# Sliding-window attention and channel mix on one core: q and k turned by VectorE in 32x32 blocks, scores on 32-row groups, outputs of batches 2 to 7 turned by the crossbar

## The chip, the cores and the metric

The kernel runs on one core of a Trainium2 chip. The metric is the device time of one execution in microseconds (us). Three runs of the kernel before gave 235.13, 235.77 and 236.39 us; the median is 235.77.

The engines that matter here are TensorE (matmuls; PE in the profile, its weight loads PEld), VectorE (DVE), ScalarE (ACT), GpSimd (POOL, which here mostly issues loads that cast from float32 to bfloat16) and SyncE (SP, which issues stores and crossbar transposes). Each engine works through its own queue in order.

## What is computed

```python
# q, k, v: (8 batches, 8 heads, 576, 64) float32
scores = matmul(q, k.T) / sqrt(64)
rel    = pos[:, None] - pos[None, :]
bias   = 2.0 ** -(head + 1) * -abs(rel)
scores = where((rel >= 0) & (rel < 128), scores + bias, -1e9)
attn   = softmax(scores)
x      = matmul(attn, v)            # heads laid side by side: (8, 576, 512)
xp     = x moved down by one position, zero first
xk     = mu_k * x + (1 - mu_k) * xp
xr     = mu_r * x + (1 - mu_r) * xp
out    = sigmoid(xr @ w_r) * (relu(xk @ w_k) ** 2 @ w_v)    # 512 -> 1024 -> 512
```

## The kernel before, in words

All matmuls take bfloat16. The work has two halves that are interleaved: attention per batch b and head pair g (8 x 4), and the channel mix, which takes two batches P = b // 2 at a time (1,152 rows in chunks of 512, 384 and 256).

**Attention of one head pair.** A matmul contracts over partitions, so q and k are needed with the 64 head values on partitions, and they come from memory with positions on partitions. How they are turned depends on the batch:
- Batches 1 and 2: wide loads into `cb` (L463), 32 transposes of 64x64 blocks by TensorE per head pair into two PSUM banks (`qk_quad`, L1053), and two copies from PSUM to `qk` (L663, on ScalarE or VectorE).
- Batches 3 to 5: eight loads of one 128-position block each per batch, four for q and four for k (L498), transposes for two head pairs at a time (`qk_some` through `halves`, L804), and four copies on ScalarE.
- Batches 6 and 7: the same loads, then crossbar transposes issued by SyncE into `qx` (`flip`, L502).
- Positions 512 to 575 (the tails) are loaded apart into `ts` (L488) and turned by TensorE for batches 1 to 3 (L879, then a copy on VectorE) and by the crossbar from batch 4 on (`tail_flip`, L595).

Then `scores` (L693) computes, for the two heads of the pair, the scores of each key block against the queries that can see it. Each head lies on 64 partitions, so the two heads run on the two 64-row halves of the array. A pair gives two PSUM tiles `duo` of two banks (both that there are). ScalarE takes the exponential (L707), VectorE multiplies by a stored mask that holds bias and window (L720). `attend` (L749) multiplies by v, with a column of ones that gives the sums; VectorE takes the reciprocal (L755) and scales (L760) into `xu`, of which there are three.

**Turning the output.** The mix needs channels on partitions. For batches 0 to 5 TensorE transposes `xu` (`out_t`, L787) and ScalarE copies to `xt` (L663). For batches 6 and 7 SyncE issues a crossbar transpose from `xu` to `xt` (`out_flip`, L869). `shift` then forms on VectorE the difference of neighbours `dl` (L847) and the two mixes `xk` and `xr` (L854).

**Channel mix** (`channel_mix`): xk times w_k (L958), relu on ScalarE (L965), square (L931 on VectorE; for the first three chunks L929 on ScalarE is allowed too), xr times w_r (L976), tanh on ScalarE for the sigmoid (L983), the squares times w_v (L992), the product on VectorE (L997), and a store by SyncE (L1022).

**What sets the order.** The kernel's Python code holds a planner (class `Plan`): every step is a node with engines, an estimated duration, priorities, and buffers that it takes and frees. The planner plays the schedule through and the instructions are emitted in the order that it finds. So a change of one step moves many others on every queue. `rank` makes the priorities from tables (`LEAD`, `SHIFT`), `WAIT` holds back transposes on 64-row halves, and `XRL`, `AHEAD` and `SLOPE` pace attention against the mix. In `pe_key`, steps on the same array split are drawn together.

Of the kernel before, what the change touches and what calls it, by code (L numbers as in the profile page):

```python
# [33 lines left out]
class Plan:  # L34
# [63 lines left out]
    def pe_key(self, n, rows):  # L98
        key = n.prio["PE"] if isinstance(n.prio, dict) else n.prio
        if rows == 64 and n.rows[0] == 64:  # L100
# [82 lines left out]
def kernel(  # L183
# [30 lines left out]
    NQ, NA, NX, NV, NC = 4, 4, 3, 2, 2  # L214
    XB = range(6, B)
    XO = range(6, B)
    X0 = 16
# [6 lines left out]
    WIDE = (1, 2)  # L224
    PART_WIDE = True
    QK1 = (ACT, DVE)
    TW = (0,)
    QUAD = 0.040
    RUN = {2: 64 * 284 / 345.0, NF: 128 * 284 / 390.0}
# [5 lines left out]
    WAIT = 7.42  # L235
    COST = {'first': 1.28, 'v': 1.15, 'q': 0.944, 'ts': 0.66, 'tv': 0.58, 'w': 0.88, 'run4': 1.0, 'run2': 1.03, 'flip': 1.0, 'mu': 1.0, 'x': 1.0}
    SS = ()
    OH = ()
    QM = 2
    OM = 0  # L240
# [4 lines left out]
    def SQ(order):  # L245
        return (DVE, ACT) if order < 3 else (DVE,)
# [7 lines left out]
    XTT = range(4, B)  # L254
    MMASK = False
    VDEP = 1
    TCOST = 1.5
    KLAST = 1
# [13 lines left out]
    ts_buf = many(2, [128, H, D], BF16, "ts")  # L272
    tt_buf = many(2, [128, G, 3, 64], BF16, "tt")
    qk_buf = many(NQ, [128, 2, SM], BF16, "qk")
    qx_buf = many(2, [128, 2, G, SM], BF16, "qx")
    half_buf = qx_buf[0].rearrange("p i g s -> p (i g s)").rearrange(
        "p (a i r h d) -> p a i r h d", a=2, i=2, r=2, d=D)
    part_buf = qx_buf[0].rearrange("p i g s -> p (i g s)")[:, 2048:4096].rearrange(
        "p (i h r d) -> p i h r d", i=2, r=2, d=D)
    wide_buf = [c.rearrange("p i r h d -> p (i r h d)").rearrange(  # L280
        "p (i h r d) -> p i h r d", i=2, r=NF, d=D) for c in cb_buf]
    stage = qx_buf[1].rearrange("p i g s -> p (i g s)").bitcast(FP32).rearrange(
# [36 lines left out]
    plan = Plan(dict(qx=2, p2=2, p1=N1, pt=4 - N1, qk=NQ, at=NA, xu=NX, vs=NV, cb=NC, ts=2, tt=2, xt=2, dl=2, dl0=4,  # L319
# [10 lines left out]
    def dve_t(n, fast=1):  # L330
# [4 lines left out]
        PE: (19.41, 21.75, 20.3, 20.77, 27.74, 12.48, 14.5, 17.35, 11.67, 21.63),  # L335
        ACT: (-36.25, -14.3, 13.52, -0.46, 8.81, -1.54, 38.45, -38.45, -6.19, 11.9),
        DVE: (-3.5, -13.64, -11.95, 8.63, -28.73, 12.81, 21.66, -2.46, -14.09, 3.03),
# [3 lines left out]
        PE: {(0, 0): 33.45, (1, 0): 0.96, (2, 0): 26.3, (3, 0): 24.3, ('fkk',): -39.43, ('p1', 'fkk'): 4.02, ('p1', 'fxk'): 5.15},  # L341
        ACT: {(1, 0): -17.87, (2, 0): 20.9, (3, 0): 41.7, ('frl',): 48.19, ('rl', 'fp1'): 40.97, ('rs', 'fp1'): -20.02},
        DVE: {(0, 0): -69.5, (1, 0): 89.05, (1, 1): -21.81, (1, 2): -35.86, (2, 0): -19.05, (3, 0): -5.03, ('fp1', 'frs'): -11.82, ('frl',): -102.36, ('ot', 'fp1', 'frs'): 6.45},
# [98 lines left out]

    def blanks(after):
# [8 lines left out]
        for t in range(2):  # L452
            late(tt_buf[t][:, :, 2], 0.0, 0.17)
# [22 lines left out]
    def tail_load(b):  # L476
# [3 lines left out]
        if b in TW:  # L480
            for i in range(2):
                ns.append(dma(POOL, 104, issue_t(128), lambda e, i=i: nc.gpsimd.dma_start(
                    out=ts_buf[h.idx].rearrange("p h d -> p (h d)")[:, 256 * i:256 * i + 256],
                    in_=(q, k)[i][b, :, SM:S].rearrange("h (c r) d -> h c (r d)", r=4)), [g], kind="ts"))
            return h, ns
        for i in range(2):
            src = (q, k)[i][b, :, SM:S].rearrange("h p d -> p h d")
# [813 lines left out]
```

## Time and profile before

| What | Value |
|---|---|
| median of three runs | 235.77 us (235.13 to 236.39) |
| span of the profiled execution | 233.9 us |
| runs' median above the span | 1.9 us |
| granted TensorE clock | 1.000 |
| last score matmuls of batch 7 start | 179.2 us |
| last attention matmuls of batch 7 end | some 184.2 us |
| last `xu` of batch 7 ends | 188.2 us |
| loads by GpSimd (software queue) | 96,016 packets, 16.26 MB |
| crossbar transposes | 16 of q and k, 4 of tails, 8 of outputs |

The page does not list a time of its own for the profiled execution; it gives the span, from the first to the last instruction, and the runs' times lie 1.2 to 2.5 us above it.

How to read it: the page gives the busy share of each engine, a row of forty digits per engine (each the busy tenth of a fortieth of the span), the chain of work that ended last, and groups of instructions. Behind each group stands the idle time of its engine just ahead of it and what ended that. Three longer answers of the trace are used: a table of busy times in stretches, TensorE's instructions in order of time, and groups kept apart by shape.

### The profile page before, as it was taken

The numbers are of one execution on the slowest core, as the hardware profiler recorded it, in microseconds if no ns is written. First come the engines' busy times: TensorE is split into PE (matmuls) and PEld (weight loads), VectorE is DVE, ScalarE is ACT, GpSimd is POOL, SyncE is SP. The second block draws the span as 40 slices with busy tenths as digits, with TensorE's granted clock in tenths as the row PEclk, the third lists the DMA queues.
The fourth block names the chain that finished last, engine by engine and source line by source line (L and its number), as shares of the span: only waits on it lengthen the run. The fifth ranks groups of instructions, "written<-read, shape, count | busy, mean of one in ns | idle before, by whom it ended". The sixth has DMA issues, their size and how long they took to land.

```text
span 233.9 us, 6461 instructions
## 1 busy us (share of the span) xinstructions
PE 225.3 (96%) x2586; PEld 138.3 (59%) x2615; DVE 189.6 (81%) x424; ACT 164.7 (70%) x294; POOL 93.5 (40%) x120
## 2 busy tenths in 40 slices
PE   8999799999999999999999999979999999999994
PEld 7676666665756755555855765535564744445462
DVE  7497998999998999887999999879899965324252
ACT  3769998979986969979997585845674626236261
POOL 8796655679972980794195740000000000000000
PEclk9999999999999999999999999999999999999999
DMA  7999999999999999899999999952314121121212
GB/s 172 184 163 193 187 170 201 193 172 192 157 143 126 145 143 179 70 163 175 127 189 108 180 158 206 169 93 92 118 32 121 69 76 45 46 90 48 90 45 90
DMA packets 121565, 31.09 MB, mean 133 GB/s; under 512 B 108216, under 2 KB 117696, under 8 KB 121536
## 3 DMA queue, kind: packets, MB, share of 16 engines
q0 software_dynamic: 96016, 16.26, 97.6%
q1 hardware_dynamic: 23776, 13.84, 27.0%
q10 hardware_dynamic: 1744, 0.59, 1.1%
q8 instruction: 20, 0.33, 0.6%
q14 instruction: 9, 0.07, 0.1%
HBM read 33.56 MB, written 9.44 MB: 184 GB/s over the span
## 4 chain that ended last, share of the span: by engine, by line
PE 75%; DMA 13%; DVE 4%; ACT 3%; issue 2%; POOL 1%; POOLq 0%; DVEq 0%; ACTq 0%
PE uno L992 25%; PE uno L958 21%; PE uno L976 12%; PE duo L749 6%; PE duo L693 5%; DMA ts<-in_k_dram 4%; DMA xt<-xu 3%; DMA wk_sb<-in_moe_w_k_dram 3%; DMA vs<-in_v_dram 3%; PE uno L787 3%; ACT at L707 2%; PE uno L1053 1%; PE uno L804 1%; DVE kk L931 1%; POOL vs L467 1%
## 5 line engine op out<-in xcount | busy, mean ns | idle before, releaser
L992 PE MATMUL uno<-wv_sb,kk 128*128 128x512 bf16 (+2 forms) x277 | 70.8, 373 | 1.5 <-DVE kk L931 0.5
L707 ACT ACTIVATE at<-duo 128x1024 bf16<-128x1024 f32 (+2 forms) x68 | 63.9, 986 | 8.5 <-PE duo L693 8.5
L958 PE MATMUL uno<-xk,wk_sb 128*128 128x256 bf16 (+2 forms) x412 | 69.1, 313 | 0.6
L965 ACT ACTIVATE rl<-uno 128x256 bf16<-128x256 f32 (+2 forms) x104 | 46.8, 481 | 13.3 <-PE uno L958 11.5
L958 PEld LDWEIGHTS <-wk_sb 128*128 128x128 bf16 x416 | 38.5, 98 | 20.2 <-issue 0.2
L983 ACT ACTIVATE rs<-uno 128x512 bf16<-128x512 f32 x36 | 21.7, 606 | 34.5 <-PE uno L976 32.5
L992 PEld LDWEIGHTS <-kk 128*128 128x128 bf16 x296 | 26.8, 98 | 28.3 <-DVE kk L931 1.3
L997 DVE SCALAR_TENSOR_TENSOR ot<-rs,uno 128x512 f32<-128x512 bf16 (+2 forms) x37 | 24.8, 669 | 19.7 <-PE uno L992 16.3
L467 POOL DMA_DIRECT2D vs<-in_v_dram x32 | 28.4, 903 | 28.7 <-PE duo L749 21.3
L720 DVE TENSOR_TENSOR at<-at,mask 128x1024 bf16<-128x1024 bf16 x56 | 37.3, 684 | 2.2 <-ACT at L707 2.0
L976 PE MATMUL uno<-wr_sb,xr 128*128 128x512 bf16 x138 | 36.7, 379 | 0.9 <-DVE ot L997 0.5
L931 DVE TENSOR_TENSOR kk<-rl 128x256 bf16<-128x256 bf16 (+2 forms) x96 | 31.3, 340 | 7.6 <-ACT rl L965 6.2
L854 DVE SCALAR_TENSOR_TENSOR xr<-dl,mu_sb,xt 128x576 bf16<-128x576 bf16 (+1 forms) x32 | 24.9, 779 | 0.3
L854 DVE SCALAR_TENSOR_TENSOR xk<-dl,mu_sb,xt 128x576 bf16<-128x576 bf16 (+1 forms) x32 | 24.6, 778 | 0.0
L749 PEld LDWEIGHTS <-at 128*128 128x128 bf16 x576 | 21.5, 98 | 5.1 <-issue 0.6
L663 ACT COPY qk<-uno 128x512 bf16<-128x512 bf16 (+1 forms) x40 | 21.3, 598 | 3.4 <-PE uno L1053 1.7
L760 DVE TENSOR_TENSOR xu<-duo,rc 128x640 bf16<-128x640 f32 x28 | 22.7, 819 | 0.2
L976 PEld LDWEIGHTS <-xr 128*128 128x128 bf16 x144 | 13.5, 98 | 15.9 <-issue 0.7
L498 POOL DMA_DIRECT2D cb<-in_k_dram x20 | 17.7, 922 | 5.0 <-DMA vs<-in_v_dram 3.2
L749 PE MATMUL duo<-vs,at 128*128 128x65 bf16 x448 | 19.1, 194 | 0.1
L498 POOL DMA_DIRECT2D cb<-in_q_dram x20 | 17.8, 924 | 1.7 <-DMA cb<-in_k_dram 0.7
L663 ACT COPY xt<-uno 128x576 bf16<-128x576 bf16 (+2 forms) x28 | 15.9, 578 | 2.4 <-PE uno L787 2.3
(81 smaller groups left out, 209.1 us busy)
## 6 DMA issues: line engine op xcount, KB each, us to landing
out_dram<-ot SPq DMA_DIRECT2D x30, 256.0 KB, 5.5
vs<-in_v_dram POOLq DMA_DIRECT2D x32, 128.0 KB, 7.6
cb<-in_q_dram POOLq DMA_DIRECT2D x20, 128.0 KB, 6.8
cb<-in_k_dram POOLq DMA_DIRECT2D x20, 128.0 KB, 7.5
out_dram<-ot SPq DMA_DIRECT2D x10, 128.0 KB, 1.7
wk_sb<-in_moe_w_k_dram POOLq DMA_DIRECT2D x2, 512.0 KB, 7.6
cb<-in_q_dram POOLq DMA_DIRECT2D x4, 256.0 KB, 10.0
cb<-in_k_dram POOLq DMA_DIRECT2D x4, 256.0 KB, 10.3
```

The source lines that it names most:

```text
L467: return dma(POOL, 256, issue_t(1024), lambda e: nc.gpsimd.dma_start(out=vs_buf[h.idx][:, j, :, 0:D], in_=v[b, :, 128 * j:128 * j + 128].r ...
L498: return [dma(POOL, 256, issue_t(1024), lambda e, r=r: nc.gpsimd.dma_start(out=cb_buf[h.idx][:, i, r], in_=src[:, :, r]), [g], kind="q") f ...
L663: (nc.scalar.copy if e == ACT else nc.vector.tensor_copy)(out=out, in_=in_)
L707: lambda e, ah=ah, w=w, hp=hp: nc.scalar.activation(out=ah(), in_=two(hp)[:, :, 0:w], func=AF.Exp, scale=float(scale)), (), [hp])
L720: nc.vector.tensor_tensor(out=a, in0=a, in1=m, op=ALU.mult)
L749: nc.tensor.matmul(a[:, hl, t - t0], lhsT=at[:, lo:lo + 128], rhs=vs[:, u, 2 * g + hl, :] if u < NF else tvb[:, 2 * g + hl], start=(u == u ...
L854: lambda e: nc.vector.scalar_tensor_tensor(out=buf[hk.idx][:, g, e0 + c0:e0 + c1], in0=dls(), scalar=mu[:, g:g + 1], in1=xc(1), op0=ALU.mu ...
L931: nc.vector.tensor_tensor(out=out, in0=in_, in1=in_, op=ALU.mult)
L958: nc.tensor.matmul(one(hp)[:, 0:n], lhsT=wk_sb[:, po, 128 * fo:128 * fo + 128], rhs=xk_buf[hx.idx][:, po, c0:c1], start=(po == 0), stop=(p ...
L965: a = op(ACT, act_t(n), [s], pr, lambda e, hp=hp, hr=hr: nc.scalar.activation(out=rl_buf[hr.idx][:, 0:n], in_=one(hp)[:, 0:n], func=AF.Rel ...
L976: nc.tensor.matmul(one(hp), lhsT=xr_buf[hx.idx][:, po, 128 * c:128 * c + 128], rhs=wr_sb[:, po], start=(po == 0), stop=(po == NPO - 1))
L992: nc.tensor.matmul(one(hv)[:, a:b], lhsT=kk_buf[hk.idx][:, fo, o:o + 128], rhs=wv_sb[:, fo, a:b], start=(fo == 0), stop=(fo == NFO - 1))
```

## The change

**q and k of batches 1 to 7.** One load takes four heads (`quad_load`): partition 32 h + p holds 18 consecutive positions of head h with all 64 values, 4,608 bytes in a row in memory. VectorE transposes 32x32 blocks of 4-byte elements (`turn`), each element being two neighbouring bfloat16 values. The result `qt` has, per head, 32 partitions; each holds pairs of values, and position is the free index. Tails need no steps of their own.

**Scores** (`scores4`). Four heads at a time on four groups of 32 rows; the 64 values are contracted in two passes (t = 0 and 1, every second element), the second adding to the first in PSUM. One step covers half of the key blocks for four heads and again fills both `duo` tiles. The exponential and the mask product keep their shapes and counts.

**Outputs.** The crossbar turns `xu` for batches 2 to 7 instead of 6 and 7 only.

**Squares.** `SQ` allows ScalarE for every chunk instead of for three.

**Planner.** New tables `LEAD` and `SHIFT`, `WAIT` 17.59 instead of 7.42, and steps on 32-row groups are drawn together as those on 64-row halves are.

In the built programs, VectorE has 28 block transposes (L1061), 32 squares (96 before) and 3 + 4 copies of q and k from PSUM (6 + 5 before); ScalarE has 72 squares (8 before), 4 copies of 576 columns to `xt` (20 before) and 1 + 4 copies of q and k (38 + 3 before); TensorE has 560 matmuls for the scores of batches 1 to 7 (L1084; 336 before); SyncE's queue holds 24 crossbar transposes (28 before).

```diff
@@ constants
-    XB = range(6, B)
-    XO = range(6, B)
+    XO = range(2, B)
+    TB = S // 32
+    KW = 128 * NJ
...
-    WAIT = 7.42
+    WAIT = 17.59
...
     def SQ(order):
-        return (DVE, ACT) if order < 3 else (DVE,)
+        return (DVE, ACT)
...
@@ buffers
-    cb_buf = many(NC, [128, 2, NF, H, D], BF16, "cb")
+    raw_buf = many(NC, [128, 2, 2, TB * D], BF16, "raw")
+    qt_buf = many(NT, [128, S + KW, 2], BF16, "qt")
...
@@ loads
+    def quad_load(b, i, c, h, g):
+        src = (q, k)[i][b, 4 * c:4 * c + 4].rearrange("h (p r) d -> (h p) (r d)", r=TB)
+        return dma(POOL, QUADKB, issue_t(128), lambda e: nc.gpsimd.dma_start(
+            out=raw_buf[h.idx][:, i, c], in_=src), [g], kind="quad")
...
-    def flip(b, i, j, g):
-        return dma(SPE, FLIP * RATE, FISSUE, lambda e: nc.sync.dma_start_transpose(
-            out=qx_buf[xbh[b].idx][:, i, :, 128 * j:128 * j + 128],
-            in_=cb_buf[ch[b].idx][:, i, j].rearrange("p h d -> p (h d)")),
-            [g, (cl[b][NF * i + j], FWAIT)], (), [ch[b]], FLAT, True)
...
+    def turn(b, c):
+        hq, n, res = Hold("qt"), None, []
+        for i in (1, 0):
+            def emit(e, i=i):
+                nc.vector.transpose(
+                    out=qt_buf[hq.idx][:, S * i:S * i + S].rearrange("p s t -> p (s t)").bitcast(FP32)
+                    .rearrange("p (q t) -> p t q", t=TB),
+                    in_=raw_buf[ch[b].idx][:, i, c].bitcast(FP32).rearrange(
+                        "p (t w) -> p t w", w=32))
...
+    def scores4(b, c, half, hq, has, deps):
+        pieces, m0 = (QUAD0, QUAD1)[half]
...
+            for (u, q0, n) in pieces:
+                c0 = BASE[u] + q0 - 128 * u - a0
+                for t in range(2):
+                    for j in range(4):
+                        r = 32 * j
+                        nc.tensor.matmul(
+                            two(hps[j // 2])[:, j % 2, c0:c0 + n],
+                            lhsT=qt[r:r + 32, S + 128 * u:S + 128 * u + 128, t],
+                            rhs=qt[r:r + 32, q0:q0 + n, t],
+                            start=(t == 0), stop=(t == 1), skip_group_check=True)
...
@@ main loop, batches 1 to 7
-        htt, n_tt = tails(b, (0, b, 0, 0))
-        for g in range(G):
...
+        for c in range(2):
+            hq, y = turn(b, c)
+            has = [Hold("at"), Hold("at")]
+            s0, m0 = scores4(b, c, 0, hq, has, y)
+            s1, m1 = scores4(b, c, 1, hq, has, y + [(s0, 0.0)])
+            for j in range(2):
+                g = 2 * c + j
+                prio = (0, b, 0, g)
+                r, hx = attend(b, g, 0, NJ, has[j], [m0[j], m1[j]] + vl[b], prio)
+                if b in XO:
+                    xks[b, g], xrs[b, g] = shift(b, g, 0, S, out_flip(b, g, r, hx, xth[b]),
+                                                 (0, b, 0, g + XD), xh[P], xth[b])
```

More of the change, by code (lines that the diff above doesn't have):

```diff
@@ L99, in pe_key @@
         key = n.prio["PE"] if isinstance(n.prio, dict) else n.prio
-        if rows == 64 and n.rows[0] == 64:
+        if rows != 128 and n.rows[0] == rows:
             return (-1e8,) + tuple(key)
@@ L223 @@
     RATE = 284.0
[L224 to L227, printed above, removed]
     QUAD = 0.040
-    RUN = {2: 64 * 284 / 345.0, NF: 128 * 284 / 390.0}
+    RUN = {2: 64 * 284 / 345.0}
+    QUADKB = 576 * 284 / 390.0
     FLIP = 1.0
@@ L451, in blanks @@
             late(tv_buf[t][0:64, :, D], 1.0)
-        for t in range(2):
-            late(tt_buf[t][:, :, 2], 0.0, 0.17)
+        late(tt_buf[0][:, :, 2], 0.0, 0.17)
+        n_pad.extend(dve_op(0.1, lambda e, t=t: nc.vector.memset(qt_buf[t][:, 2 * S:S + KW], 0.0),
+                            [after], (0, 31)) for t in range(NT))
         for t in range(NA):
@@ L922 @@
     of = out.rearrange("b s m -> (b s) m")
-    n_hw = 39 + sum(4 if g in FT else 2 for g in range(3)) + 8 * len(XB) + len(XTT) + G * len(XO)
+    n_hw = 39 + sum(4 if g in FT else 2 for g in range(3)) + G * len(XO)
     n_split = -n_hw % 8
@@ L1060, in qk_quad @@
         w = 64 * nr
[L1061 removed]
+        ys = [op(QK0, {ACT: act_t(2 * w), DVE: dve_t(2 * w)}, [t], prio + (3,),
                  lambda e, r=r: copy_any(
```

265 lines of the change are left out of this document (62 added, 203 removed).

## The prediction

> **What bounds the kernel now.** I read the page's busy shares and slices first, then a table of stretches, then TensorE's instructions in order of time, then VectorE's groups by shape.
>
> ```profile
> PE 225.3 (96%) x2586; PEld 138.3 (59%) x2615; DVE 189.6 (81%) x424; ACT 164.7 (70%) x294; POOL 93.5 (40%) x120
> ...
> PE   8999799999999999999999999979999999999994
> ...
> DVE  7497998999998999887999999879899965324252
> ...
> DMA  7999999999999999899999999952314121121212
> ```
>
> TensorE is busy in nearly every slice, and the chain that ended last is 75% TensorE: from about 28 us on, TensorE sets the end. But VectorE's digits are 9 in most slices up to the twenty-fourth (some 140 us) and fall only in the last quarter. The DMA engines are full as long as there are loads.
>
> ```profile
> 0.00:30.00 30.00, 27.70 (x493) 20.60 (x495) 23.20 (x89) 21.99 (x49) 22.12 (x34) 1.00 1.54 179
> 30.00:100.00 70.00, 68.92 (x970) 43.79 (x984) 66.59 (x133) 61.95 (x110) 46.96 (x57) 1.00 1.83 157
> 100.00:150.00 50.00, 49.58 (x583) 30.83 (x586) 47.28 (x95) 40.34 (x65) 24.44 (x30) 1.00 1.97 161
> 150.00:188.20 38.20, 36.65 (x327) 21.11 (x330) 34.24 (x71) 22.07 (x37) 0.00 (x0) 1.00 0.37 93
> 188.20:233.90 45.70, 42.44 (x225) 21.92 (x227) 18.26 (x40) 18.36 (x35) 0.00 (x0) 1.00 0.19 67
> ```
>
> The columns are the stretch, then the busy time of TensorE, weight load, VectorE, ScalarE and GpSimd, the granted clock (1.00 throughout), the DMA share and GB/s. I cut at 188.2, where VectorE finishes the last attention output (xu). Up to there VectorE is busy 23.20 + 66.59 + 47.28 + 34.24 = 171.3 us and idle 16.9, of which 6.8 lie in the first 30 us. Between 30 and 150 it is busy 113.87 of 120, 94.9%. So there are two nearly full engines while attention runs; after 188.2 only TensorE is full (VectorE 18.26 of 45.70). ScalarE has room: 102.3 of 120.
>
> **TensorE's side.** A matmul's displayed length contains its drain, so I price a step by the distance to the next instruction's start.
>
> ```profile
> 46.22 0.45 PE L1053 MATMUL uno<-ident,cb 64*64 64x64 bf16 x32
> 46.60 1.04 PE L976 MATMUL uno<-wr_sb,xr 128*128 128x512 bf16 x3
> ...
> 48.25 0.44 PE L787 MATMUL uno<-ident,xu 128*128 128x128 bf16 x5
> 48.53 1.03 PE L992 MATMUL uno<-wv_sb,kk 128*128 128x512 bf16 x4
> ...
> 51.11 0.56 PE L693 MATMUL duo<-qk 64*128 64x256 bf16 x8
> ...
> 51.66 1.04 PE L992 MATMUL uno<-wv_sb,kk 128*128 128x512 bf16 x4
> ...
> 60.73 0.64 PE L804 MATMUL uno<-ident,cb 64*128 64x64 bf16 x32
> 61.30 0.82 PE L958 MATMUL uno<-xk,wk_sb 128*128 128x384 bf16 x4
> ```
>
> The columns are start, length, instruction and count. The 32 small transposes of L1053 take 46.60 - 46.22 = 0.38 us (the eight groups lie between 0.37 and 0.50, mean 0.42); the 32 of L804 0.57; five output transposes (L787) 0.28; the scores of one head pair (L693, twelve matmuls) 0.55. The four tail transposes of L879 take 0.22 by the same reading.
>
> Removed: 8 groups of L1053 x 0.42 = 3.4; 6 of L804 x 0.57 = 3.4; 3 of L879 x 0.22 = 0.7; output transposes of batches 2 to 5, 16 x 0.28 = 4.5. Sum **12.0 us**.
>
> Replaced: 28 groups of L693 on 64-row halves by 28 on 32-row quarters. A 512-column matmul advances TensorE by 0.216 us (27 of them in 5.83 on the chain). An old group streams 1,024 columns with two heads side by side, 0.43 us, and takes 0.55, so 0.12 is switching and filling. A new group covers half the sequence for four heads, each contracted in two passes of 32 rows: again 1,024 columns if four run side by side, 0.43 + 0.12 = 0.55. No row of this trace has 32-row groups. Bounds: 0.43 (no switching) and, if only two overlap, 0.86 + 0.12 = 0.98. I take 0.55, since L1053's four small tiles at once come near to full overlap: 32 x 64 columns / 4 stream in 0.22, plus 0.12 is 0.34, against 0.37 to 0.50 measured. Net for TensorE: -12.0, so 233.9 - 12.0 = **222 us if TensorE alone decides**.
>
> The Trainium skill speaks against a full draw: "TensorE: Matmul & The Clock Gate", section "Part 3: Packing small matmuls", gives 3.07 times for four row tiles, so a new group would by my estimate take 0.43 x 4 / 3.07 + 0.12 = 0.68, in all 28 x 0.13 = 3.6 us more. No run here shows it yet.
>
> **VectorE's side.**
>
> ```profile
> L760 DVE TENSOR_TENSOR xu<-duo,rc 128x640 bf16<-128x640 f32 x28 | 22.7, 819 | 0.2
> L854 DVE SCALAR_TENSOR_TENSOR xr<-dl,mu_sb,xt 128x576 bf16<-128x576 bf16 x28 | 22.7, 812 | 0.3
> ...
> L847 DVE TENSOR_TENSOR dl<-xt 128x576 bf16<-128x576 bf16 x28 | 12.3, 448 | 3.7 <-DMA xt<-xu 3.2 <-ACT xt L663 0.4
> ```
>
> The columns after the shapes are count, busy time, mean ns, idle time before. Added: 28 block transposes of 128x576 four-byte elements. No such row exists. The nearest that pass one element per cycle cost 0.819 (640 f32 elements) and 0.812 (576); the lower bound is 0.448 (576 elements at the two-byte rate), the upper two passes, 1.62. I take **0.81**: 28 x 0.81 = 22.7.
>
> Removed, counted from the instructions queued on each engine in the two programs: 28 squares of 256 columns (0.286), 19 of 384 (0.351) and 17 of 512 (0.419), which go to ScalarE, 21.8 in all; three copies of 512 (0.686), one of 256 (0.42), three of the tails (0.42), 3.7 in all. So VectorE loses 25.5 and gains 22.7: the cover for the transposes is what ScalarE takes over. Up to the last xu the means add up to 196.7 before (386 instructions) and 191.1 after (343). Neighbours overlap: 196.7 shown against 171.3 busy is 0.066 each. So 191.1 - 343 x 0.066 = 168.5 busy: only **2.8 us less on VectorE against 12.0 on TensorE**. VectorE becomes the tighter engine while attention runs.
>
> When does attention end, then? The first 30 us stay (23.2 busy). The other 145.3 take 153 us at the 94.9% of before, ending at 183.1; with no idle time, 175.3. I take 97%, between them, because the squares' waits for ScalarE (6.2 us) mostly leave VectorE: 30 + 145.3 / 0.97 = 179.8. Before, the last attention matmuls ended at 184.2, 4 us ahead of the last xu; 4 ahead again is 175.8. Behind them the old trace has 233.9 - 184.2 = 49.7 us, all TensorE and a tail. In the new queue TensorE has 1.3 us less behind that point (columns and counts priced as above: 45.0 against 46.3). So 175.8 + 48.4 = 224.2, plus 1 us for late crossbar transposes (below): 225.2.
>
> **ScalarE** loses 37 copies of qk (0.616, 22.8 us) and 16 of xt (0.65, 10.4) and gains the 64 squares: 28 x 0.453 + 19 x 0.564 + 17 x some 0.67 (from the two shorter ones) = 34.8. About even, with idle time of 18 us between 30 and 150 as cover; if that were gone its 1.6 us would count.
>
> **Loads and queues.** 40 + 8 + 14 q and k loads on GpSimd's queue (some 0.92, 0.75 and 0.71 each, 52 us) become 28 with source runs of 4,608 bytes instead of 256 or 1,024 (0.75 each by the wide loads' row, 21 us). I cost this at nothing: GpSimd waited 21.3 us for free v buffers, so it is ahead anyway. On SP's queue 16 crossbar transposes of q and k and 4 of tails go; 16 of outputs come, 1.2 us of issue each, in front of output stores. The eight old ones land in 2.4 us on quiet engines and 7.7 under loads; VectorE then waits at dl, the head of its queue, with masks and xu behind, and TensorE's attention behind those. Between xu and dl the new VectorE queue holds 5 to 16 us of work in batches 2 to 5 (5.2, 7.6, 5.2 and 6.8 for batch 2). If all land at 7.7, the waits add up to some 8 us (2.9 twice, 2 once, shorter ones); at 2.4 to none. I take 1.
>
> **Forecast.** 225.2 span; the median of the runs shown, 235.77, is 1.9 above the traced span of 233.9. So 225.2 + 1.9 = **227.1, say 227.0 us**.
>
> **Rivals.**
> - TensorE alone stays the bound: 222 + 1.9 = 224. For it: it is full now. Against: VectorE's 2.8. Chance 0.14.
> - The 32-row groups stretch. L1053 takes up to (0.42 - 0.12) / 0.22 = 1.4 times its streaming; 0.43 x 1.4 + 0.12 = 0.72, 28 x 0.17 = 4.8 more, of which VectorE's slack hides about 2: 230. The skill's figure above falls inside this. Chance 0.11.
> - Output transposes land late under loads: VectorE waits 8 instead of 1: 234. For it: 7.7 us under load in the old trace; against: fewer packets now. Chance 0.09.
> - **Slower:** the block transpose takes two passes, 1.62. VectorE up to the last xu then has 168.5 + 28 x 0.81 = 191.2; 30 + 168 / 0.97 = 203.2, attention ends 199.2, the end 247.6, time 249.5. Decides from where attention ends past 233.9 - 48.4 = 185.5, the last xu past 189.5: (159.5 x 0.97 - 145.3) / 28 = 0.34 more, 1.15 us each. For it: VectorE has no spare time; against: the f32 rows run one element per cycle. Chance 0.14, with times between 236 and 250.
> - That the change isn't made as said can be left out: the queues hold the 28 block transposes and 24 crossbar ones.
>
> **How the numbers follow.** My case has 0.48: from TensorE alone (224) to VectorE at its old 94.9% (183.1, 3.3 later: 230). The rest, 0.04, is unnamed. The range 221 to 238 leaves out what is below TensorE's bound and the upper part of the slow case. Faster by over 0.5% (about what a measurement of this kernel can tell from no change): own case, the first two rivals and a little of the third, 0.74; within 0.5%: most of the third, 0.09; slower: 0.17.
>
> **What would show it.** Block transposes near 0.8 us; score groups 0.55 apart; VectorE above 95% between 30 and 175 us and TensorE with some 5 us more idle there, released by VectorE (xu, at, dl); 45 us of nearly unbroken TensorE at the end. Wrong if the transposes exceed 1.15 us, if score groups are 0.7 or more apart, if dl waits on xt transposes for more than 5 us, or if TensorE has no new idle time (then 224).

## The result, and the profile after

The kernel after takes 245.25 us (median of 4 runs, 243.71 to 246.83) against 235.45 for the kernel before (234.89 to 236.39): a ratio of 1.0425, 95% interval 1.0363 to 1.0487. It is slower, and outside the predicted range. The profiled execution has a span of 242.7 us. Here and below the ratios leave out single executions that took clearly longer than the others of the same kernel (one of small_loads took 758 us).

From the page of the kernel after, the lines that answer to those of before:

```profile
PE 220.7 (91%) x2299; PEld 128.2 (53%) x2299; DVE 196.6 (81%) x383; ACT 164.2 (68%) x306; POOL 58.2 (24%) x86
...
PE   8999788999935999999799996978999999999994
...
DVE  7677999999647899999799987979999996333433
...
PEclk9999999999995799999999999999999999999999
DMA  7999999999994999199917994592343321122123
```

TensorE is busy for less time (220.7 against 225.3), but there are holes in it, the largest at the twelfth and thirteenth digit, where VectorE has a hole too; the granted clock falls at the thirteenth and fourteenth. The table of stretches of the kernel after:

```profile
0.00:30.00 30.00, 27.19 (x413) 19.39 (x417) 24.11 (x84) 20.13 (x42) 20.00 (x32) 1.00 1.45 180
30.00:100.00 70.00, 61.27 (x674) 36.24 (x667) 61.44 (x104) 51.49 (x99) 21.22 (x31) 0.93 1.38 161
100.00:150.00 50.00, 45.11 (x510) 25.09 (x507) 45.60 (x78) 37.77 (x67) 12.75 (x18) 1.00 0.98 135
150.00:188.20 38.20, 36.04 (x417) 20.26 (x406) 36.73 (x65) 28.75 (x48) 4.22 (x5) 1.00 0.61 86
188.20:242.70 54.50, 51.06 (x309) 27.27 (x307) 28.75 (x56) 26.05 (x53) 0.00 (x0) 1.00 0.22 79
```

Between 30 and 150 us both engines have idle time: TensorE 13.6 of 120 us, VectorE 13.0, of which 4.7 us fall on the same moments. Before it was 1.5 and 6.1. So neither is full there, and something else holds them up. The waits of the kernel after name it (who waited for whom: us in total, times, longest):

```profile
DVE dl L773 <- DMA xt<-xu: 8.0, 4, 5.4
...
PE duo L709 <- DVE at L1111: 4.9, 2, 4.6
...
DVE ot L899 <- DMA out_dram<-ot: 3.8, 2, 2.3
```

VectorE waits for the crossbar transposes of the output: 7.7 of its 13.0 idle us between 30 and 150 end with one. The view of the instructions of line 795, which issue them, gives the time from issue to landing:

```profile
DMA to landing us min/median/max: 2.4/6.4/15.1
```

Before, the same line (of eight transposes) read:

```profile
DMA to landing us min/median/max: 2.4/2.4/7.7
```

The largest wait, in VectorE's order of time (start, length, and in brackets the idle time ahead and what ended it):

```profile
64.10 0.68 DVE L1111 TENSOR_TENSOR at<-at,mask 128x1024 bf16<-128x1024 bf16 x1
70.21 0.46 DVE L773 TENSOR_TENSOR dl<-xt 128x576 bf16<-128x576 bf16 x1 [5.43 <-DMA xt<-xu]
70.59 0.69 DVE L1111 TENSOR_TENSOR at<-at,mask 128x1024 bf16<-128x1024 bf16 x1
```

and TensorE's order at the same place:

```profile
73.75 0.62 PE L709 MATMUL duo<-vs,at 128*128 128x65 bf16 x8 [4.63 <-DVE at L1111]
...
76.57 1.01 PE L860 MATMUL uno<-xk,wk_sb 128*128 128x256 bf16 x4 [2.04 <-DVE ot L899]
```

The mask products (L1111) stand behind dl in VectorE's queue, and TensorE's attention stands behind the mask products. One late transpose stops both engines.

Two of the change's own prices, from VectorE's groups by shape and from TensorE's order of time in the kernel after:

```profile
L1061 DVE STREAM_TRANSPOSE qt<-raw 128x576 f32<-128x576 f32 x28 | 33.7, 1241 | 0.0
```

```profile
51.78 0.64 PE L1084 MATMUL duo<-qt 32*128 32x256 bf16 x24
52.35 0.82 PE L894 MATMUL uno<-wv_sb,kk 128*128 128x512 bf16 x3
```

A block transpose takes 1.24 us where 0.81 was forecast, 12 us more on VectorE in all. The 24 score matmuls on 32-row groups take 52.35 - 51.78 = 0.57, as forecast (0.55).

### The profile page after: what moved, and what is told of

The parts are those of the page before. It is cut to its first block, busy times and chain, and to the rows that moved or that the text cites. A ratio compares the mean times of both kernels' runs of the same rounds, so it can differ in the third digit from the quotient of the medians.

```text
span 242.7 us, 5792 instructions
## 1 busy us (share of the span) xinstructions
PE 220.7 (91%) x2299; PEld 128.2 (53%) x2299; DVE 196.6 (81%) x383; ACT 164.2 (68%) x306; POOL 58.2 (24%) x86
## 2 busy tenths in 40 slices
DMA packets 71675, 31.06 MB, mean 128 GB/s; under 512 B 59352, under 2 KB 63712, under 8 KB 71648
## 3 DMA queue, kind: packets, MB, share of 16 engines
q0 software_dynamic: 46832, 16.26, 64.4%
## 4 chain that ended last, share of the span: by engine, by line
PE 41%; DVE 26%; DMA 14%; issue 12%; ACT 3%; POOL 2%; DVEq 0%; ACTq 0%; POOLq 0%
PE uno L894 12%; PE uno L860 12%; DMA out_dram<-ot 7%; DVE qt L1061 6%; PE uno L878 5%; DVE at L1111 5%; DVE xu L720 4%; DMA raw<-in_q_dram 4%; DVE ot L899 4%; PE uno L614 3%; DMA xt<-xu 3%; DVE xk L780 2%; PE duo L1084 2%; DVE xr L780 2%; PE duo L640 2%
## 5 line engine op out<-in xcount | busy, mean ns | idle before, releaser
L860 PE MATMUL uno<-xk,wk_sb 128*128 128x256 bf16 (+2 forms) x416 | 75.8, 320 | 9.1 <-DVE ot L899 7.5
L1101 ACT ACTIVATE at<-duo 128x1024 bf16<-128x1024 f32 x56 | 54.8, 1036 | 8.6 <-PE duo L1084 8.5
L860 PEld LDWEIGHTS <-wk_sb 128*128 128x128 bf16 x416 | 39.8, 100 | 37.5 <-issue 11.6
L1111 DVE TENSOR_TENSOR at<-at,mask 128x1024 bf16<-128x1024 bf16 x56 | 36.5, 676 | 0.0
L831 ACT ACTIVATE kk<-rl 128x256 bf16<-128x256 bf16 (+2 forms) x72 | 34.7, 510 | 0.6
L878 PE MATMUL uno<-wr_sb,xr 128*128 128x512 bf16 x144 | 34.7, 379 | 0.0
L1061 DVE STREAM_TRANSPOSE qt<-raw 128x576 f32<-128x576 f32 x28 | 33.7, 1241 | 0.0
L709 PE MATMUL duo<-vs,at 128*128 128x65 bf16 x448 | 19.4, 196 | 5.4 <-DVE at L1111 4.9
L780 DVE SCALAR_TENSOR_TENSOR xr<-dl,mu_sb,xt 128x576 bf16<-128x576 bf16 (+1 forms) x32 | 23.8, 763 | 0.0
L833 DVE TENSOR_TENSOR kk<-rl 128x256 bf16<-128x256 bf16 (+2 forms) x32 | 10.9, 341 | 14.3 <-ACT rl L867 14.0
L1084 PE MATMUL duo<-qt 32*128 32x256 bf16 (+2 forms) x560 | 18.5, 250 | 2.8 <-DVE xu L720 1.6
L773 DVE TENSOR_TENSOR dl<-xt 128x576 bf16<-128x576 bf16 (+1 forms) x32 | 13.5, 434 | 8.2 <-DMA xt<-xu 8.0
## 6 DMA issues: line engine op xcount, KB each, us to landing
raw<-in_k_dram POOLq DMA_DIRECT2D x14, 288.0 KB, 10.5
wv_sb<-in_moe_w_v_dram POOLq DMA_DIRECT2D x2, 512.0 KB, 11.7
```

The costliest lines, as they stand in the source:

```text
L709: nc.tensor.matmul(a[:, hl, t - t0], lhsT=at[:, lo:lo + 128], rhs=vs[:, u, 2 * g + hl, :] if u < NF else tvb[:, 2 * g + hl], start=(u == u ...
L780: lambda e: nc.vector.scalar_tensor_tensor(out=buf[hk.idx][:, g, e0 + c0:e0 + c1], in0=dls(), scalar=mu[:, g:g + 1], in1=xc(1), op0=ALU.mu ...
L831: nc.scalar.activation(out=out, in_=in_, func=AF.Square)
L860: nc.tensor.matmul(one(hp)[:, 0:n], lhsT=wk_sb[:, po, 128 * fo:128 * fo + 128], rhs=xk_buf[hx.idx][:, po, c0:c1], start=(po == 0), stop=(p ...
L878: nc.tensor.matmul(one(hp), lhsT=xr_buf[hx.idx][:, po, 128 * c:128 * c + 128], rhs=wr_sb[:, po], start=(po == 0), stop=(po == NPO - 1))
L1061: nc.vector.transpose(out=qt_buf[hq.idx][:, S * i:S * i + S].rearrange("p s t -> p (s t)").bitcast(FP32) .rearrange("p (q t) -> p t q", t=TB),
```

## The experiments

Two theories: **late landing** (the crossbar transposes of outputs land late while loads run, and VectorE's queue stands behind them) and **dear transposes** (1.24 us on a VectorE with no room). A third possibility is that the turn itself, or the new order, loses. All kernels are the kernel after with the edit shown, unless another is named.

### What a block transpose costs: forms, price81

Edit of forms: 36 VectorE instructions appended behind the last step, six each of six forms.

> The changed kernel with 36 VectorE instructions on 576 four-byte elements added behind its end, six of each of six forms: the block transpose as used (output 72 bytes apart), the same with dense output, with strided input and dense output, a two-byte block transpose of 1,152 elements, a copy with the strided output, a copy with dense output. If the strided write makes the block transpose cost 1.24 us, the dense form takes some 0.8 us and the strided copy is also slow; if the transpose itself costs it, the dense form takes 1.24 as well; if other traffic costs it, all forms here are near 0.8, since nothing else runs.

VectorE's groups by shape, of forms (in order: 2-byte transpose; 4-byte transpose with a strided input; with a strided output, as in the kernel after; dense; copy with a strided output; dense copy):

```profile
L1163 DVE STREAM_TRANSPOSE qt<-raw 128x1152 bf16<-128x1152 bf16 x6 | 8.3, 1378 | 0.2
L1160 DVE STREAM_TRANSPOSE qt<-raw 128x576 f32<-128x576 f32 x6 | 7.5, 1258 | 0.2
L1154 DVE STREAM_TRANSPOSE qt<-raw 128x576 f32<-128x576 f32 x6 | 7.5, 1257 | 0.2
L1157 DVE STREAM_TRANSPOSE qt<-raw 128x576 f32<-128x576 f32 x6 | 4.7, 779 | 0.2
L1166 DVE COPY qt<-raw 128x576 f32<-128x576 f32 x6 | 4.2, 708 | 0.2
L1169 DVE COPY qt<-raw 128x576 f32<-128x576 f32 x6 | 2.8, 460 | 0.2
```

With nothing else running, the dense transpose takes 0.78 and the one whose neighbours lie 72 bytes apart 1.26. So it is the distance that costs, on either side and for a copy too, not the transposing and not traffic beside it. The forecast's 0.81 holds for the dense form alone.

price81 was to make the instruction cheaper in place:

```diff
-                nc.vector.transpose(
+                src = raw_buf[ch[b].idx][:, i, c].bitcast(FP32).rearrange("p (t w) -> p t w", w=32)
+                nc.vector.tensor_tensor(
...
-                    in_=raw_buf[ch[b].idx][:, i, c].bitcast(FP32).rearrange(
-                        "p (t w) -> p t w", w=32))
+                    in0=src, in1=src, op=ALU.max)
```

> The changed kernel, same order on every queue, with each block transpose replaced by an elementwise maximum of the same 576 four-byte elements with the same addresses (q and k are not turned, so the output is not the reference's). It should take some 0.8 us instead of 1.24. Theory price (the 28 x 0.43 = 12 us too much on VectorE make the loss): the time falls by 10 to 14 us, to 231 to 235. Theory landing (late output transposes and stores make the loss): it falls by less than 5, above 240.

price81 takes 245.62 us, a ratio of 1.0396 (1.0307 to 1.0484). This tells nothing on the price: its maximum has the same strided output and takes as long, so the expected 0.8 us was not tested. VectorE's group, of price81:

```profile
L1062 DVE TENSOR_TENSOR qt<-raw 128x576 f32<-128x576 f32 x28 | 33.3, 1227 | 0.1
```

It was a miss in the design, which forms explains.

### Take the lateness away: small_flips, small_loads, small_loads2

small_flips, the transposes of batches 2 to 5 cut to one of five blocks:

```diff
-            out=xt_buf[ht.idx][:, g, X0:X0 + 128 * NJ].rearrange("p (t c) -> p t c", c=128),
-            in_=xu_buf[hx.idx].rearrange("p t h d -> p (t h d)")))
+            out=xt_buf[ht.idx][:, g, X0:X0 + 128 * (1 if b < 6 else NJ)].rearrange("p (t c) -> p t c", c=128),
+            in_=xu_buf[hx.idx][:, 0:(1 if b < 6 else NJ)].rearrange("p t h d -> p (t h d)")))
```

> The changed kernel, same order on every queue, in which the output transposes of batches 2 to 5 move only the first of five 128x128 blocks (the rest of xt keeps old data, so the output is not the reference's). Theory landing: VectorE's waits at dl (8.0 us) and most of those for stores vanish, 233 to 239. Theory price: 243 or more, since VectorE's own work stays.

small_flips takes 233.58 us, a ratio of 0.9931 (0.9889 to 0.9974), which is 11.7 us off the kernel after. Time to landing and the wait of dl for xt, of small_flips:

```profile
DMA to landing us min/median/max: 2.2/5.0/9.5
```

```profile
DVE dl L773 <- DMA xt<-xu: 2.1, 3, 1.4
```

The lateness is not all gone: the median landing is still 5.0. The longest ones are gone (9.5 instead of 15.1 us), and with them most of the waiting (2.1 instead of 8.0). Stretches of small_flips:

```profile
30.00:100.00 70.00, 64.60 (x746) 38.28 (x750) 68.06 (x116) 57.86 (x110) 25.87 (x37) 1.00 1.24 155
100.00:150.00 50.00, 47.56 (x524) 27.02 (x533) 48.54 (x84) 39.28 (x70) 12.38 (x18) 1.00 0.92 119
```

VectorE is now busy (68.06 + 48.54) / 120 = 97.2% there, the share that the forecast took, and the clock stays at 1.00.

small_loads cuts the other party, the loads of batches 3 to 7, to a quarter of their bytes (those of v in the same way, two heads of eight); the 24 transposes are whole.

```diff
-            out=raw_buf[h.idx][:, i, c], in_=src), [g], kind="quad")
+            out=raw_buf[h.idx][:, i, c, 0:(TB * D if b < 3 else 288)],
+            in_=src[:, 0:(TB * D if b < 3 else 288)]), [g], kind="quad")
```

> The changed kernel, order kept, with the loads of q, k and v of batches 3 to 7 cut to a quarter of their bytes (old data in the rest, not the reference's output); output transposes stay whole. If they land late because loads share the DMA engines with them: median landing falls from 6.4 to near 2.4 us and the time to 231 to 237. If they are late by themselves (their own number, or the stores beside them): landing stays above 5 and the time above 241.

small_loads takes 229.73 us, a ratio of 0.9779 (0.9741 to 0.9816), somewhat below the expected 231 to 237. small_loads2 is the same kernel, run once more for its trace.

> The kernel after with the loads of q, k and v of batches 3 to 7 cut to a quarter of their bytes, once more, for its trace; what is left out of the loads makes the result not the reference's. It gave 229.7. If the late crossbar transposes come from sharing the queues' engines with the loads, the time from issue to landing of the transposes of the output is near 2.4 us in the median instead of 6.4, and the waits of dl for xt are 2 us or less in sum instead of 17. If they are late because of the crossbar itself (24 transposes with the stores behind them), the median stays at 5 or more and the gain came from elsewhere.

It takes 229.78 us. (The waits of dl for xt in the kernel after add up to 8.0 us, not to the 17 of this expectation.) Time to landing, then stretches, of small_loads2:

```profile
DMA to landing us min/median/max: 2.4/2.7/5.5
```

```profile
30.00:100.00 70.00, 67.02 (x782) 39.22 (x781) 69.83 (x119) 59.84 (x114) 25.87 (x40) 1.00 0.95 125
100.00:150.00 50.00, 49.31 (x547) 27.61 (x540) 50.00 (x86) 39.58 (x70) 9.25 (x14) 1.00 0.49 90
```

With the loads thinned the transposes land in 2.7 us instead of 6.4, dl waits for xt once, for 0.3 us, and VectorE is full (119.83 of 120). The transposes are late because of the loads beside them, not because there are 24. This kernel has the order, the score groups and the 1.24 us of the kernel after and is 2.2% faster than before, so in this order none of these three makes a loss by itself. (The kernel before was not run with thinned loads; what it would gain by them is not shown.)

### One part alone: before_xo, turn_alone

before_xo is the kernel *before* with `XO = range(2, B)`, planned anew.

> The kernel before with one part of the change alone: outputs of batches 2 to 5 turned by the crossbar, with its planner's old tables. Theory landing: these 16 transposes stand under loads, VectorE waits at dl, 240 or more. Theory price: TensorE loses 4.5 us of transposes, ScalarE 10 us, the time stays within 232 to 238.

before_xo takes 240.54 us, a ratio of 1.0228 (1.0158 to 1.0298): the output transposes cost some 5 us on a kernel without block transposes. Waits of before_xo:

```profile
DVE dl L847 <- DMA xt<-xu: 12.6, 6, 3.2
```

turn_alone is the kernel after with `XO = range(6, B)`, planned anew with the same tables.

> The changed kernel with the outputs of batches 2 to 5 turned by TensorE again, as before, and copied by ScalarE; planned anew with the same tables. Theory landing: 231 to 237, although the block transposes still take 1.24 us. Theory price: 241 or more, since VectorE's work is unchanged and TensorE has 4.5 us more.

turn_alone takes 237.51 us, a ratio of 1.0123 (1.0084 to 1.0162). That lies between the two expectations, so neither theory alone is borne out. Its transposes land in 2.5 us in the median. Stretches of turn_alone:

```profile
30.00:100.00 70.00, 66.92 (x806) 40.21 (x795) 69.83 (x120) 63.73 (x120) 27.76 (x40) 1.00 1.23 152
100.00:150.00 50.00, 48.93 (x518) 27.74 (x515) 49.93 (x82) 42.09 (x75) 6.38 (x9) 1.00 0.61 114
```

VectorE is full in 119.76 of 120 us: with no late output transposes, VectorE's own work decides, the block transposes' 1.24 us with it. Each part alone is slower than before, by 2.3% and 1.2%.

### Take the price away: dense, dense_small, turn_dense

dense lets the block transposes write their output densely, which leaves the positions in another order:

```diff
-                    .rearrange("p (q t) -> p t q", t=TB),
+                    .rearrange("p (t q) -> p t q", t=TB),
```

> The changed kernel, same order on every queue, with the block transposes writing their output densely (0.78 us in the run of the six forms against 1.26 for the form in use; positions of q and k are then permuted, so the output is not the reference's). This takes 28 x 0.46 = 13 us from VectorE, as the maximum, itself slowed by the strided write, did not. If the price counts by itself: 232 to 235. If late landings set the time and VectorE only waits longer at dl for what it saves: 239 to 245.

dense takes 240.64 us, a ratio of 1.0215 (1.0143 to 1.0288). The transpose and the wait of dl for xt, of dense:

```profile
L1061 DVE STREAM_TRANSPOSE qt<-raw 128x576 f32<-128x576 f32 x28 | 20.7, 756 | 0.1
```

```profile
DVE dl L773 <- DMA xt<-xu: 11.4, 5, 8.3
```

The transposes take 0.756, yet of the 13.6 us taken from VectorE only 4.6 come out. Some of what VectorE saves ahead of a late transpose turns into waiting: 11.4 us at dl instead of 8.0.

dense_small adds the edit of small_flips.

> Both: dense block transposes and output transposes of batches 2 to 5 that move one block of five (not the reference's output), order kept. If the price counts once landings are out of the way: 222 to 227, as forecast for 0.81 us and early landings. If it does not count at all: 232 to 235, as with small transposes alone.

dense_small takes 229.16 us, a ratio of 0.9779 (0.9726 to 0.9833): 16 us off the kernel after, with a span of 227.3 where the forecast had 225.2. It is above the expected 222 to 227, but the two causes together make up the miss but for 2 us.

The two add up, within the intervals. The dense output gains 4.6 us with late landings (245.25 to 240.64) and 4.4 without most of them (233.58 to 229.16); the smaller output transposes gain 11.7 and 11.5. So the late landings are not the main thing that keeps the other 9 of the 13.6 us (dl still waits 4.3 us for xt here). Stretches of dense_small:

```profile
30.00:100.00 70.00, 66.54 (x775) 38.75 (x766) 64.89 (x119) 59.10 (x112) 27.54 (x40) 1.00 1.26 158
100.00:150.00 50.00, 49.15 (x551) 27.70 (x541) 47.04 (x85) 39.87 (x70) 10.68 (x15) 1.00 1.00 126
```

TensorE is busy 115.7 of the 120 us (112.2 in small_flips) and VectorE 111.9 (116.6): with the price gone, TensorE is the fuller of the two.

turn_dense is turn_alone with the dense output.

> The turn alone (outputs of batches 2 to 5 turned by TensorE and copied by ScalarE, as in the kernel before) with the block transpose writing its output in one run; the scores are then computed on values in another order, so the result is not the reference's. In the run with the turn alone VectorE was busy 49.93 of 50 us from 100 to 150, at 237.5. If VectorE and the transpose's price set that time, 28 transposes at some 0.77 instead of 1.24 take 13 us off VectorE, of which TensorE lets through what it can: 226 to 231. If the loss of the turn lies in the order of steps or in the narrow score groups, 235 or more, with VectorE waiting instead.

turn_dense takes 233.92 us, a ratio of 0.9956 (0.9928 to 0.9984): 3.6 us less than turn_alone, not the 6.5 to 11.5 expected. Stretches of turn_dense:

```profile
30.00:100.00 70.00, 67.82 (x804) 40.58 (x797) 67.67 (x122) 64.80 (x123) 27.66 (x40) 1.00 1.26 159
100.00:150.00 50.00, 50.00 (x536) 28.49 (x535) 46.69 (x82) 43.66 (x77) 6.37 (x9) 1.00 0.57 105
```

The bound has passed to TensorE (50.00 of 50.00), whose busy time is 221.7 us in all: the turn by itself took only 3.6 us off it, where the forecast's terms give 3.4 + 3.4 + 0.7 = 7.5.

### Dense output in the right order: turn_p1, turn_p3

If a partition holds single positions 32 apart, instead of 18 in a row, the transposes' output is dense in the right order, but the loads' runs shrink from 4,608 to 256 bytes (768 with three positions; each load becomes four):

```diff
-        src = (q, k)[i][b, 4 * c:4 * c + 4].rearrange("h (p r) d -> (h p) (r d)", r=TB)
+            for j in range(4):
+                src = (q, k)[i][b, 4 * c + j].rearrange("(a p r) d -> p a (r d)", p=32, r=1)
```

> The turn alone with the result of the reference: positions are loaded one by one (runs of 256 bytes in memory, four loads per former load, 32 partitions each, 18 runs per partition), so that the block transpose writes dense 4-byte elements and the order of positions is right. Transpose 0.76 to 0.8. If the loads hide, as turn_dense: 226 to 231. If the many short runs delay the raw tiles, VectorE or TensorE waits for loads, and the time goes to 235 to 245.

> The same with three positions in a run (768 bytes in memory, 6 runs per partition), so that the transpose writes with a distance of 12 bytes between neighbours instead of 4 or 72. If the cost comes as soon as the output is not dense: 1.24 to 1.26 each, and a time like the turn alone, 236 to 238. If it needs a distance over 16 bytes or so: some 0.78 each, and 226 to 231.

turn_p1 takes 241.66 us, ratio 1.0260 (1.0188 to 1.0332), turn_p3 235.45, ratio 1.0013 (0.9977 to 1.0050). VectorE's groups of turn_p1, then of turn_p3:

```profile
L1068 DVE STREAM_TRANSPOSE qt<-raw 128x576 f32<-128x576 f32 x28 | 21.4, 766 | 0.8 <-DMA raw<-in_k_dram 0.8
```

```profile
L1068 DVE STREAM_TRANSPOSE qt<-raw 128x576 f32<-128x576 f32 x28 | 26.2, 947 | 0.7 <-DMA raw<-in_k_dram 0.7
```

The price falls, but the loads' queue grows from 46,832 to 109,104 and 66,096 packets, and TensorE is busy 61.37 and 65.13 of the 70 us from 30 to 100 (66.92 in turn_alone). Its longest single wait there, 4.0 and 3.8 us, is for the weights w_r, which come by the same queue; turn_alone has no such wait. In turn_p1 the loads take more than the transposes gain, in turn_p3 a part of it: it is 2 us below turn_alone, and the 0.947 us lie between the two prices that were expected.

### Does lateness cost in any order?

The planner believes that an output transpose lands early and that a block transpose takes 0.77 us. It can be told otherwise:

```diff
-    TURN = 0.1
+    TURN = 0.57
...
-        return [fab(SPE, FLIP * NJ / 4, n, FLAT, [hx], True)]
+        return [fab(SPE, FLIP * NJ / 4, n, (FLAT[0], FLAT[1] + 4.0), [hx], True)]
```

With these prices the tables (`LEAD`, `SHIFT`, `WAIT`, `SLOPE`, `XRL`, `AHEAD`) were searched again. The steps stay those of the kernel after; their order changes, and with it which engine takes some of the squares (VectorE has 32 in the kernel after, 30 in late_planned).

> The kernel after, same steps, with the planner told what the runs measured: a block transpose 0.47 us dearer (TURN 0.57) and an output transpose landing 4 us later, and with its priority tables (LEAD, SHIFT, WAIT, SLOPE, XRL) searched again for these prices. If the loss of the change is the waiting for late transposes and not the transposes themselves, an order that expects them late wins most of it back: waits of dl for xt under 3 us, and 231 to 236 (VectorE stays full because of the 1.24 us). If it can't be planned around (VectorE has nothing else to do, or the transposes get later), 240 or more.

late_planned takes 231.66 us, a ratio of 0.9861 (0.9791 to 0.9931), and no dl waits for xt. runs2_planned and runs3_planned add shorter runs in the loads (two and three positions):

> The same, with two positions in a run of the loads (512 bytes in memory, four loads of 32 partitions each in place of one), so that the block transpose writes 8 bytes apart; priced at 0.05 more than dense, tables searched. Transposes: 0.78 if one word is skipped at no cost, some 0.85 if the cost grows evenly with the distance (0.766 at 4 bytes, 0.947 at 12). With VectorE relieved and late landings planned for: 227 to 231. If the loads' short runs, some 75,000 packets, delay the raw tiles or the crossbar more than that: 233 to 238.

> The same with three positions in a run (768 bytes), transposes 0.947, fewer packets (66,000 on the loads' queue in the run turn_p3). 228 to 232 if VectorE's price and the late landings were the two losses; 234 or more, as turn_p3, if the split loads cost what the transposes gain.

runs2_planned takes 236.53 us, a ratio of 1.0020 (0.9982 to 1.0058), runs3_planned 230.55, a ratio of 0.9816 (0.9730 to 0.9903), within what was expected. In runs2_planned VectorE waits 4.7 us for raw and 3.8 for xu buffers that late transposes hold: the expected 227 to 231 failed on the loads. Its transposes, 8 bytes apart, in VectorE's groups:

```profile
L1068 DVE STREAM_TRANSPOSE qt<-raw 128x576 f32<-128x576 f32 x28 | 20.7, 758 | 4.7 <-DMA raw<-in_k_dram 4.7
```

Which of the told prices does it, or is it the search? Three kernels with about equally long searches: no price told, the landing alone, the transposes' price alone. Each is one order that one search found.

> The kernel after with its priority tables searched as long as those of late_planned, but with the planner's old prices (block transpose 0.77, output transposes landing early). If late_planned's gain came from the prices it was told, this stays near the kernel after, 240 to 248, with waits of dl for xt. If the search by itself, or any other order, gave the gain: 231 to 236.

> The same search with only the landing of the output transposes told 4 us later, the block transpose at the old price. If lateness is the main cause: 231 to 237, waits of dl for xt under 4 us, and VectorE at the bound through the 1.24 us that this plan does not know of. If the price of the transpose was what late_planned gained by: 240 or more.

> The same search with only the block transpose's price told (0.47 us more), landing as before. If lateness is the main cause, the waits of dl for xt stay at 5 us or more and the time at 237 to 244, since a plan that counts VectorE rightly still places dl soon behind the transposes. If the price was the main cause: 231 to 235.

| Kernel (steps as after) | us | Ratio to before (95%) | Landing, median | dl waits for xt |
|---|---|---|---|---|
| kernel after | 245.25 | 1.0425 (1.0363 to 1.0487) | 6.4 | 8.0 |
| searched_only | 240.97 | 1.0208 (1.0093 to 1.0323) | 5.9 | 6.3 |
| price_only | 233.21 | 0.9914 (0.9871 to 0.9957) | 3.6 | 2.6 |
| late_planned (both) | 231.66 | 0.9861 (0.9791 to 0.9931) | 2.5 | none |
| late_only | **230.00** | 0.9775 (0.9735 to 0.9815) | 6.2 | none |

The order of searched_only does not give the reference's output, though it leaves no step out. The reason is open, so as a control it is weaker than the others.

late_only gives the clearest answer, and is a little faster than the expected 231 to 237. Its time to landing and its stretches:

```profile
DMA to landing us min/median/max: 2.4/6.2/10.0
```

```profile
30.00:100.00 70.00, 65.43 (x728) 37.74 (x735) 69.24 (x120) 58.88 (x112) 27.50 (x40) 1.00 1.54 180
100.00:150.00 50.00, 48.97 (x543) 27.70 (x549) 48.09 (x81) 41.08 (x72) 10.58 (x14) 1.00 1.01 136
```

The transposes land as late as in the kernel after, but no dl waits for them: in batch 2 its queue puts some 10.5, 11.5, 11.7 and 12.3 us of VectorE work between xu and its dl, the kernel after 6.3, 9.1, 6.4 and 7.6 (counted from the queues, with the measured durations). (In batch 4 it has less than the kernel after; the kernel after's two longest waits are in batch 2.) VectorE is busy 117.3 of 120 us, and the same steps, but for one square that ScalarE takes over, are 2.2% faster than before. The last xu ends at 185.6 us, against 196.7 in the kernel after and 185.7 in small_flips: an order that expects the lateness wins back ahead of the last xu what small_flips won by taking it away.

My expectation for price_only (237 to 244) failed: 233.21 with less work between xu and dl. Its gain is of another kind. Its order gives VectorE 21 squares instead of 32 (7.0 instead of 10.9 us), and its last xu ends at 202.7, later than in the kernel after, with 30.1 us behind it instead of 46.0. Its transposes landed in 3.6 us; why an order meets fewer loads I have not shown.

## Why the prediction was wrong

The forecast ended the last xu at 179.8 us, with 45.4 behind it. The last xu and what lies behind it, by the traces:

| | Last xu ends | Behind it | Span |
|---|---|---|---|
| forecast | 179.8 | 45.4 | 225.2 |
| kernel after | 196.7 | 46.0 | 242.7 |
| small_flips | 185.7 | 46.1 | 231.8 |
| dense_small | 181.2 | 46.1 | 227.3 |
| late_only | 185.6 | 42.6 | 228.2 |

Nearly the whole error of 17.5 us lies ahead of the last xu: 16.9 us, of which 11.0 go with the lateness, 4.5 more with the stride (the distance between neighbours in the block transpose's output), and 1.4 remain. Two of the forecast's own signs of being wrong came true: block transposes above 1.15 us (1.24) and dl waiting for xt for more than 5 us (8.0).

- **Late output transposes, "I take 1": the step that failed most.** It was worth about 11. The mechanism was named, with its queue and who stands behind it, and dismissed for "fewer packets now". Packets did fall (121,565 to 71,675), but landing went from 2.4 to 6.4 in the median, since the new transposes are issued while loads run; the old eight were issued from 145.8 us on, when GpSimd had no more loads. The upper bound of 8 was too low as well: it let all land at 7.7, and the latest took 15.1; beside the 8.0 at dl, VectorE waited 1.4 for xu buffers and 3.8 for stores; and the stall took the clock down too.
- **Block transpose at 0.81: mis-sized.** 1.24; 0.78 dense. The rows it was taken from (819 and 812 ns) have dense operands, and I did not ask for the output's distance of 72 bytes. The slower rival had named 1.15 as the point from which the price decides, for another reason (two passes).
- **The two as one case: missing.** They stood as rivals with chances of their own. By the prediction's numbers together, 28 x 0.43 = 12.0 us more on VectorE end the last xu at 30 + 157.3 / 0.97 = 192.2, which is 12.4 later, and 8 instead of 1 for the lateness adds 7: 227.1 + 19.4 = 246.5; measured 245.25. The agreement is luck: the measured parts are some 4.5 for the price and 11.6 for the lateness, so the first is far too large and the second too small.
- **VectorE the tighter engine, 97% busy:** 89.2% in the kernel after (107.04 of 120), 97.2% in small_flips, but there at 1.24 us. Near the price that the forecast had (dense_small, 0.756 us), VectorE is busy 94.2% from 30 us to the last xu and TensorE 97.1%. So the step holds at the dear price only; at the forecast's own price both are nearly full, TensorE more. That the last xu of dense_small comes within 1.4 us of the forecast is in part luck.
- **Squares for transposes:** I had 2.8 us less on VectorE up to the last xu; dense_small has 166.1 against 171.3 before, 5.2 less, of which 28 x (0.81 - 0.756) = 1.5 come from the dense transpose being cheaper than 0.81. The direction is right, at the dense price.
- **TensorE -12.0:** 225.3 to 215.8 (dense_small) and 215.3 (late_only), so -9.5 to -10. Too large by a fifth. The turn gave 3.6 for 7.5, the outputs, from turn_dense to dense_small, 5.9 for 4.5. Of the 4 us missing from the turn, 2.4 are in the score groups: counted from start to the next start without idle time, the 28 groups of turn_dense take 17.6 us, those of before 15.2, since a group that pauses for ScalarE in its middle takes longer (up to 1.5 us with its pause, instead of 0.57). The rest is open; the trace of before has 29 matmuls fewer than its 2,615 weight loads and that of late_only 27 fewer than its 2,299, so their busy times may be somewhat low.
- **Score groups 0.55:** 0.57 for a group that nothing interrupts. The Trainium skill, "TensorE: Matmul & The Clock Gate", section "Part 3: Packing small matmuls", gives 3.07 times for four row tiles, from which I had estimated 0.68 by adding 0.12 for switching. That sum is not borne out here; 3.07 times alone would be 0.43 x 4 / 3.07 = 0.56, by the same estimate, and that the trace does not speak against.
- **ScalarE about even:** 164.7 to 164.2. **Loads at nothing:** right for VectorE's transposes (idle ahead of L1061: 0.0), wrong for the crossbar transposes, which land in 6.4 us beside the loads and in 2.7 beside thinned ones (small_loads2). **Behind the attention:** 45.4 forecast, 46.0 measured.

## What to carry to other kernels

Price a transfer at its landing under the traffic in which it will be issued, not at the median of its quiet cousins, and ask how much work stands between it and its reader in the reader's queue; where a planner makes the order, tell it that landing time (the same steps went from 245.25 to 230.00). Take a price for an operation only from a row with the same distance between elements. Where two rivals press on the same engine, work out the case in which both come true.

## What the runs showed of the hardware

- A VectorE pass over 576 four-byte elements per partition pays by the distance between neighbours. The block transpose takes 0.76 us at 4 and at 8 bytes, 0.95 at 12, 1.24 at 72 (turn_p1, runs2_planned, turn_p3, kernel after), with a strided input as with a strided output. The Trainium skill, "SBUF — State Buffer", section "Door 1: The DMA port swizzle (why `[64,N]` ≈ `[32,N]`)", says that lines of 16 bytes need two hits each for full bandwidth. The trace agrees: two four-byte elements in a line (8 bytes apart) cost nothing more, one and a third cost 0.19 us, one 0.48.
- The clock fell during the double stall at 69 to 76.6 us and came back only after it. Stretches of the kernel after, ten us each:

```profile
60.00:70.00 10.00, 8.90 (x99) 4.58 (x96) 4.78 (x6) 9.79 (x17) 1.06 (x2) 1.00 1.35 109
70.00:80.00 10.00, 4.22 (x41) 3.32 (x42) 8.02 (x15) 1.64 (x5) 1.84 (x3) 0.58 0.66 86
80.00:90.00 10.00, 10.00 (x115) 5.90 (x114) 8.81 (x12) 7.92 (x17) 4.52 (x7) 0.91 1.76 154
```

A wait of 4.63 and one of 2.04 us left TensorE at 0.58 of its clock in these ten us and at 0.91 in the next. In stretches of two us the clock reads 1.00 up to 70, 0.90 up to 72, 0.50 up to 80, 0.54 up to 82 and 1.00 after that. Work resumed at 76.6, so it ran some 5 us at about half clock: eight matmuls of L860 took 1.90 us at 78.51, where eight take 1.05 at 36.26. Part of a stall's price comes after it.
